# Projecting q, k and v in six chunks of 512 columns in place of eight of 384

## The chip, the core and the metric

The kernel runs on one core of a Trainium2 chip. The metric is the device time of one execution in microseconds; the times below are medians of several executions. The engines named are PE (TensorE, matmuls, with PEld for its weight loads), DVE (VectorE), ACT (ScalarE), POOL (GpSimd) and SP (SyncE), whose queue issues all the DMAs of this kernel.

## What is computed

Two mixers work on the same input x of 2048 rows by 1024 columns, in bf16, and a gate for each row mixes their results. Mixer A is a dilated local attention with 32 heads of 32 columns; each position looks at eight positions, itself and those 2, 4, ... 14 before it. Mixer B is a gated MLP with a spatial matmul.

```python
g = sigmoid((x * gate_w).sum(-1, keepdims=True))
qkv = (x @ wqkv)                       # 1024 x 3072: q, k, v of 32 heads
logits = einsum(q, k[s - 2*w]) * Dh ** -0.5,  w = 0..7, masked where s - 2*w < 0
a = (softmax(logits) applied to v[s - 2*w]) @ wo
z = gelu(x @ w_in);  z1, z2 = halves of z;  z2 = layernorm(z2)
b = (z1 * (w_sp @ z2 + b_sp)) @ w_out
out = g * a + (1 - g) * b
```

## The kernel before

**Stages on PE.** PE runs one matmul after another, in the order of the program. z2_quad and z2_tile (L223) make the first columns of z2 while x arrives. Then the projection (L431) makes q, k and v. Then the rest of z2 (L223), z1 (L473, 14 blocks f, each written out to z1_d), the spatial matmul in chunks (g_chunk, L487, 14 blocks f of 16 matmuls) and the output products (final_chunk, L509 with wo for a, L513 with w_out for b). The order of the chunks is g 0, g 1, final 0, g 2, final 1, g 3, final 2, final 3. All PE results go through one pool of eight PSUM tiles.

**The projection.** Heads are taken in eight groups of four, so a group has 128 columns each of q, k and v (C = 128). For each group g the loop at L423 goes over 16 row blocks j. A row block takes eight matmuls over kt, each 384 columns wide: q, k and v of the group next to each other in one PSUM tile. ACT casts the tile to bf16 into a stage slot (L434). After every four row blocks three DMAs (L440 to L442) store q, k and v to q_d, k_d and v_d in DRAM. The weights of a group lie in one of three slots wg_slots; a slot has four parts of 128 columns: q, k, v in the order the attention wants (columns by element, then head), and v as it was loaded. load_wg(g) loads the three blocks by three DMAs of 256 KB; v_order(g) reorders v on ACT (for the first group half on ACT, half on DVE). The weights of the next group but one are loaded when a group begins (L425), and the next group's v is reordered after row block 8.

**The attention.** It runs on DVE, group by group, while PE goes on with later stages. For a group, q, k and v are loaded back from DRAM (load_qk L309 and L310, load_v L313). Two halves jh of the rows are worked on one after the other: multiply (L266), four folds (L269) and a last add (L272) make the logits; then the soft_a part (L277 to L281), the exponential on ACT (L284), and soft_b (L287 to L291). The product with v of a group (L299, two folds L305 and L306, last add L302) runs one group later: after the logits of group g comes the product of group g-1. After the last group its own product follows. Outputs are stored to o_d in pairs of groups (store_o, L317). After the last store, wo is loaded (L357) and o_d is read back transposed, 128 rows at a time (load_oT, L360); the first such tile oT is read by the first matmul of final chunk 0.

**Other work on DVE.** Layer norm statistics (L365 to L369, with a power on POOL at L370), the normalization (L374), and in g_chunk for each f an add and a multiply on the evicted tile (L492 and L493, called a pair below; L491 is the cast on ACT before them, and three gsb slots lie between ACT and DVE). L493 reads z1c, which load_z1c (L391) loads from z1_d.

**What sets the order.** Each engine's queue and SP's queue run in the order in which the program emits instructions (`tc.manual_schedule`). A small planner, Beat, keeps a clock that each PE tile advances by its columns over 2360 a microsecond. Work for DVE is given with a start time and a length, DMAs and the exponential with a due time, and each is emitted when the clock reaches it (DVE work 3 us before, LEAD). The attention's first start is set from the length of one group's projection:

```python
QKV_US = NJ * KT * 3 * C * BEAT
beat.steps = attention_steps(beat.now + QKV_US + 10.0)
```

Loads of the attention are due at 1.0 us after the planned end of the last DVE work that reads what they overwrite, the store of o at 1.0 or 1.5 us, wo at 1.5 us and the first three oT at 8.0 us after the planned end. Other DMAs are emitted where they stand in the program: before g chunk 0, `load_z1c(0)`, the four transposing loads of w_sp for chunk 1 (load_wsp, L388), `load_z1c(1)` and w_out (L529); after g chunk 0 the four loads of w_sp for chunk 2; after g chunk 1 those for chunk 3, and then everything that is still due.

Of the kernel before, what the change touches and what calls it, by code (L numbers as in the profile page):

```python
# [13 lines left out]
P = 128  # L14
S = 2048
D = 1024
KT = D // P
NH = 32
DH = 32
HG = 4  # L20
NG = NH // HG
C = HG * DH
W = 8
NJ = 16
NJJ = NJ + 14
FH = 1792
# [4 lines left out]
EPS = 1e-5  # L31
SCALE = DH ** -0.5
WGS = 4 * KT * C
W2P = FH + 32
BEAT = 1.0 / 2360.0
LEAD = 3.0
# [4 lines left out]
CD_OFF = A_OFF + 22016  # L41
EF_OFF = CD_OFF + 19456
# [3 lines left out]
def _sub_ap(t, offset_elems, dims):  # L46
    return bass.AP(tensor=t.tensor, offset=t.offset + offset_elems, ap=[list(t.ap[0])] + [list(d) for d in dims])
# [3 lines left out]
def kernel(  # L51
# [13 lines left out]
    nc = tc.nc  # L65
# [10 lines left out]
    def reg(off, n):  # L76
        return arena[:, off:off + n]

    q_d = dpool.tile([NG, S, C], BF, name="q_d")
    k_d = dpool.tile([NG, S + 16, C], BF, name="k_d")  # L80
    v_d = dpool.tile([NG, S + 16, C], BF, name="v_d")
# [51 lines left out]
    ob_slots = [reg(A_OFF + 11264 + r * 1024, 1024) for r in range(3)]  # L133
    asb_slots = [reg(A_OFF + 14336 + r * 1024, 1024).bitcast(F32) for r in range(2)]
    w2 = reg(CD_OFF, KT * W2P).rearrange("p (k c) -> p k c", k=KT)
    stage_slots = [reg(CD_OFF + 14848 + r * 1536, 1536).rearrange("p (j c) -> p j c", j=4) for r in range(3)]
    wg_slots = [reg(EF_OFF + r * WGS, WGS).rearrange("p (t k c) -> p t k c", t=4, k=KT) for r in range(3)]
    junk = reg(EF_OFF + 3 * WGS, FH)
    w1_slots = [reg(EF_OFF + r * 4096, 4096).rearrange("p (k c) -> p k c", k=KT) for r in range(2)]
    z1s_slots = [reg(EF_OFF + 8192 + r * 2048, 2048).rearrange("p (c t) -> p c t", c=4) for r in range(2)]  # L140
    wsp_slots = [reg(CD_OFF, 8192).rearrange("p (i a t) -> p i a t", i=16, a=4),
# [7 lines left out]
    wq_v = A_wqkv.rearrange("(k p) c -> p k c", p=P)  # L149
# [5 lines left out]
    sync = nc.sync  # L155
# [37 lines left out]

    beat = Beat()

    def load_w(g, slot):
        part = 2 if slot == 3 else slot
        sync.dma_start(wg_slots[g % 3][:, slot, :, :], wq_v[:, :, part * D + g * C:part * D + (g + 1) * C])

    def load_wg(g):  # L200
        for slot in (3, 0, 1):
            load_w(g, slot)

    def v_order(g):
        wgt = wg_slots[g % 3]
        vdst = wgt[:, 2, :, :].rearrange("p k (d h) -> p k d h", d=DH, h=HG)
        vsrc = wgt[:, 3, :, :].rearrange("p k (h d) -> p k d h", h=HG, d=DH)
        if g == 0:
            nc.scalar.copy(vdst[:, 0:4], vsrc[:, 0:4])
            nc.vector.tensor_copy(vdst[:, 4:8], vsrc[:, 4:8])  # L210
        else:
            nc.scalar.copy(vdst, vsrc)

    def z2_tile(i, c):
        N = ZW[c] + 1 if c == 3 else ZW[c]
# [103 lines left out]
    def attention_steps(t):  # L319
        beat.at(t - 8.0, lambda: load_qk(0))  # L320
        beat.at(t - 7.9, lambda: load_v(0))
        for g in range(NG):
            for took, fn in qk_steps(0) + qk_steps(1):
                yield t, took, fn
            t = beat.vector
            if g + 1 < NG:
                beat.at(t + 1.0, lambda g=g: load_qk(g + 1))
            yield t, 2.4, soft_a
            t = beat.vector
            beat.at(t + (1.0 if g == 0 else 5.0), soft_exp)  # L330
            if g == 0:
                t += 5.0
            else:
                for took, fn in pv_steps(g - 1, 0) + pv_steps(g - 1, 1):
                    yield t, took, fn
                t = beat.vector
                if g + 1 < NG:
                    beat.at(t + 1.0, lambda g=g: load_v(g))
                else:
                    load_v(g)  # L340
                if g % 2 == 0:
                    beat.at(t + 1.5, lambda g=g: store_o(g - 1))
            yield t, 2.3, soft_b
            t = beat.vector
        for took, fn in pv_steps(NG - 1, 0) + pv_steps(NG - 1, 1):
            yield t + 5.0, took, fn
        t = beat.vector
        beat.at(t + 1.0, lambda: store_o(NG - 1))
        beat.at(t + 1.5, load_wo)
        for a in range(3):  # L350
            beat.at(t + 8.0, lambda a=a: load_oT(a))
# [46 lines left out]
        sync.dma_start(w2[:, kt, 0:2 * ZC], win_v[:, kt, FH:FH + 2 * ZC])  # L398
    for i in range(2, 16):
        if i == 14:  # L400
            load_w(0, 3)
            load_w(0, 0)
        sync.dma_start_transpose(xT[:, :, i * P:(i + 1) * P], x2[i * P:(i + 1) * P, :])
    load_w(0, 1)
    load_wg(1)
    for t_d in (k_d, v_d):
        sync.dma_start(bass.AP(tensor=t_d.tensor, offset=t_d.offset, ap=[[16, P], [(S + 16) * C, NG], [1, 16]]), zeros[:])
# [6 lines left out]
    for i in range(2, 16):  # L414
        if i == 14:
            v_order(0)
        z2_tile(i, 0)

    QKV_US = NJ * KT * 3 * C * BEAT
    beat.steps = attention_steps(beat.now + QKV_US + 10.0)  # L420

    stg = 0
    for g in range(NG):  # L423
        wgt = wg_slots[g % 3]
        if 0 < g and g + 1 < NG:  # L425
            load_wg(g + 1)
        for j in range(NJ):
            ps = psum.tile([P, 512], F32, name="ps", tag="ps")
            for kt in range(KT):
                lhsT = _sub_ap(xT_flat, kt * S + j, [[NJ, P]])  # L430
                nc.tensor.matmul(ps[:, 0:3 * C].rearrange("p (t c) -> p t c", t=3), lhsT, wgt[:, 0:3, kt, :],  # L431
                                 start=(kt == 0), stop=(kt == KT - 1))
            st = stage_slots[stg % 3]
            nc.scalar.copy(st[:, j % 4, :], ps[:, 0:3 * C])  # L434
            if j % 4 == 3:
                j0 = j - 3
                dq = bass.AP(tensor=q_d.tensor, offset=q_d.offset + (g * S + j0) * C, ap=[[NJ * C, P], [C, 4], [1, C]])
                dk = bass.AP(tensor=k_d.tensor, offset=k_d.offset + (g * (S + 16) + 16 + j0) * C, ap=[[NJ * C, P], [C, 4], [1, C]])
                dv = bass.AP(tensor=v_d.tensor, offset=v_d.offset + (g * (S + 16) + 16 + j0) * C, ap=[[NJ * C, P], [C, 4], [1, C]])
                sync.dma_start(dq, st[:, :, 0:C])  # L440
                sync.dma_start(dk, st[:, :, C:2 * C])
                sync.dma_start(dv, st[:, :, 2 * C:3 * C])  # L442
                stg += 1
            if j == 8 and g + 1 < NG:
                v_order(g + 1)
            beat.run(KT * 3 * C)

    load_w1(0)
    load_w1(1)
# [14 lines left out]
    for f in range(NF):  # L464
        ch = f // 4
# [4 lines left out]
        for c in range(4):  # L470
            ps = psum.tile([P, 512], F32, name="ps", tag="ps")
# [103 lines left out]
```

## Time and profile before

| | |
|---|---|
| Time, median of 3 runs | 716.57 us (716.35 to 716.60) |
| The profiled execution: time | 716.54 us |
| Its span | 714.7 us, granted clock 0.999 |
| PE busy | 706.6 us, 99% |
| DVE busy | 414.0 us, 58% |
| ACT busy | 251.3 us, 35% |
| L431, the projection on PE | 1024 matmuls of 128x384, 166.6 us busy |
| L487, the spatial matmul on PE | 128x512, 877 records, 192.9 us busy |
| L434, the casts of the projection on ACT | 128 of 128x384, mean 480 ns |
| L491, the casts of the spatial matmul on ACT | 56 of 128x512, mean 586 ns |
| ACT waiting for L431 | 87.2 us in 109 waits |
| Loads of wqkv | 24 of 256 KB, 4.6 us to landing |
| Stores of q, k, v | 32 each of 128 KB, 2.1, 2.2 and 2.5 us to landing |
| Loads of q, k, v for the attention | 512, 960 and 960 KB, 4.9, 6.8 and 5.4 us to landing |

The span is what the profiler saw between the first and the last instruction; the execution's time is 1.8 us longer. Times within a trace are counted from the span's start. A row of a group has the engine, the operation, what it writes and reads, the number of instructions, and then the busy time and the mean length of one. A matmul's mean length is its latency in the pipeline, so the distance between matmuls is read from busy time or from pieces of the chain. Some matmul records are missing (877 of 896 here). In the chain of work, a piece has its start, its length and the number of instructions in it. In a timeline the last bracket has the idle time before an instruction and what ended it. In rows on DMAs the last figure is the time from issue to landing.

### The profile page before, as it was taken

The page shows a single profiled execution, that of the slowest core. Times are in us where ns is not written, and L with a number is a line of the kernel's source. Part 1 is how long each engine was busy: PE and PEld are TensorE (multiplying, and loading weights), DVE is VectorE, ACT ScalarE, POOL GpSimd, SP SyncE. Part 2 cuts the span into 40 slices and gives each one's busy share as a digit, 9 for nine tenths or more (in the row PEclk, how much of TensorE's full clock was granted, in tenths as well). Part 3 has the DMA queues.
Part 4 walks back from the last instruction along what each step waited for, and adds up shares of the span by engine and source line. Part 5 has one row for each costly group of instructions (what it writes and reads, how often), then busy time and mean ns, then how long its engine had stood idle before and what let it go on. Part 6 is the DMA issues. An engine that isn't in the chain of part 4 may idle for free.

```text
span 714.7 us, 8897 instructions
## 1 busy us (share of the span) xinstructions
PE 706.6 (99%) x3577; PEld 402.0 (56%) x3628; DVE 414.0 (58%) x429; ACT 251.3 (35%) x483; POOL 11.0 (2%) x23
## 2 busy tenths in 40 slices
PE   8999999999999999999999999999999999999998
PEld 4488888888865554444444444444444444444444
DVE  0000989999999999999997999211222112221111
ACT  4444454445379894353521211111111111121111
POOL 1000000000000102000000000000000000000000
PEclk9999999999999999999999999999999999999999
DMA  9967776667781206954569580772400213002310
GB/s 238 191 149 220 165 200 170 167 133 193 202 237 66 85 1 181 253 184 137 173 196 293 213 174 2 220 146 59 133 1 0 55 49 119 1 1 59 60 45 29
DMA packets 176761, 92.93 MB, mean 130 GB/s; under 512 B 145104, under 2 KB 166992, under 8 KB 176208
## 3 DMA queue, kind: packets, MB, share of 16 engines
q1 hardware_dynamic: 176720, 92.36, 48.9%
q8 instruction: 28, 0.46, 0.3%
q14 instruction: 13, 0.11, 0.0%
HBM read 47.71 MB, written 28.38 MB: 106 GB/s over the span
## 4 chain that ended last, share of the span: by engine, by line
PE 98%; DMA 1%; issue 0%; SPq 0%; DVE 0%; DVEq 0%
PE ps L487 27%; PE ps L431 23%; PE ps L223 14%; PE ps L473 13%; PE psb L513 13%; PE psa L509 8%; DMA arena<-in_B_w_in_dram 1%; SPq L396 0%; DVE arena L517 0%; DVEq L517 0%
## 5 line engine op out<-in xcount | busy, mean ns | idle before, releaser
L487 PE MATMUL ps<-arena 128*128 128x512 bf16 x877 | 192.9, 379 | 1.0
L431 PE MATMUL ps<-arena 128*128 128x384 bf16 x1024 | 166.6, 326 | 0.0
L431 PEld LDWEIGHTS <-arena 128*128 128x128 bf16 x1024 | 147.6, 144 | 18.9
L487 PEld LDWEIGHTS <-arena 128*128 128x128 bf16 x896 | 87.7, 98 | 105.7
L513 PE MATMUL psb<-arena 128*128 128x512 bf16 (+1 forms) x455 | 101.3, 372 | 0.3
L223 PE MATMUL ps<-arena 128*128 128x512 bf16 (+1 forms) x501 | 96.7, 352 | 1.8 <-DMA arena<-in_B_w_in_dram 1.2
L517 DVE SCALAR_TENSOR_TENSOR arena<-psb,omg,arena 128x512 bf16<-128x512 f32 (+1 forms) x33 | 24.3, 735 | 125.4 <-PE psb L513 113.4
L473 PE MATMUL ps<-arena 128*128 128x512 bf16 x439 | 96.4, 379 | 0.5
L266 DVE TENSOR_TENSOR arena<-arena 128x8192 bf16<-128x8192 bf16 x16 | 70.8, 4423 | 43.1 <-DMA arena<-k_d 42.8
L434 ACT CAST arena<-ps 128x384 bf16<-128x384 f32 x128 | 60.5, 480 | 90.2 <-PE ps L431 87.2
L491 ACT CAST arena<-ps 128x512 bf16<-128x512 f32 x56 | 32.8, 586 | 163.4 <-PE ps L487 136.9
L269 DVE TENSOR_TENSOR arena<-arena 128x4096 bf16<-128x4096 bf16 (+1 forms) x64 | 77.7, 1214 | 1.9
L223 PEld LDWEIGHTS <-arena 128*128 128x128 bf16 x512 | 50.1, 98 | 48.0 <-issue 1.3
L513 PEld LDWEIGHTS <-arena 128*128 128x128 bf16 x462 | 45.2, 98 | 51.5
L473 PEld LDWEIGHTS <-arena 128*128 128x128 bf16 x448 | 43.9, 98 | 52.6
L299 DVE TENSOR_TENSOR arena<-arena,att_A 128x8192 bf16<-128x8192 bf16 x16 | 70.7, 4422 | 0.2
L492 DVE TENSOR_TENSOR arena<-arena 128x512 bf16<-128x512 bf16 x56 | 23.6, 422 | 77.9 <-ACT arena L491 77.9
L516 ACT ACTIVATE arena<-psa,g_s 128x512 f32<-128x512 f32 (+1 forms) x33 | 22.2, 674 | 122.3 <-PE psa L509 118.2
L509 PE MATMUL psa<-arena 128*128 128x512 bf16 (+1 forms) x259 | 60.2, 372 | 0.4
L475 ACT ACTIVATE arena<-ps 128x512 bf16<-128x512 f32 x56 | 33.1, 596 | 55.5 <-PE ps L473 49.3
L509 PEld LDWEIGHTS <-arena 128*128 128x128 bf16 x264 | 25.8, 98 | 29.7
L228 ACT ACTIVATE arena<-ps 128x512 bf16<-128x512 f32 (+1 forms) x64 | 34.2, 538 | 23.4 <-PE ps L223 22.1
(54 smaller groups left out, 254.0 us busy)
## 6 DMA issues: line engine op xcount, KB each, us to landing
arena<-k_d SPq DMA_DIRECT2D x8, 960.0 KB, 6.8
arena<-v_d SPq DMA_DIRECT2D x8, 960.0 KB, 5.4
z_d<-arena SPq DMA_DIRECT2D x14, 512.0 KB, 3.3
arena<-z_d SPq DMA_DIRECT2D x4, 1792.0 KB, 7.5
arena<-in_A_wqkv_dram SPq DMA_DIRECT2D x24, 256.0 KB, 4.6
arena<-in_B_w_in_dram SPq DMA_DIRECT2D x4, 1024.0 KB, 7.2
q_d<-arena SPq DMA_DIRECT2D x32, 128.0 KB, 2.1
k_d<-arena SPq DMA_DIRECT2D x32, 128.0 KB, 2.2
```

What stands on the lines that cost most here:

```text
L223: nc.tensor.matmul(ps[:, 0:N], xT[:, kt, i * P:(i + 1) * P], w2[:, kt, ZC * c:ZC * c + N], start=(kt == 0), stop=(kt == KT - 1))
L228: nc.scalar.activation(z2[:, i, ZC * c:ZC * c + n], ps[:, 0:n], ACT.Gelu_apprx_tanh, accum_out=s1[:, 4 * i + c:4 * i + c + 1])
L266: TT(prod.rearrange("p (w j c) -> p w j c", w=W, j=8, c=C), in0, in1, ALU.mult)
L269: return lambda: TT(pv[:, :, 0:half], pv[:, :, 0:half], pv[:, :, half:2 * half], ALU.add)
L299: TT(prod.rearrange("p (w j d h) -> p w j d h", w=W, j=8, d=DH, h=HG), in0, in1, ALU.mult)
L431: nc.tensor.matmul(ps[:, 0:3 * C].rearrange("p (t c) -> p t c", t=3), lhsT, wgt[:, 0:3, kt, :], start=(kt == 0), stop=(kt == KT - 1))
L434: nc.scalar.copy(st[:, j % 4, :], ps[:, 0:3 * C])
L473: nc.tensor.matmul(ps[:], w1[:, kt, (f % 4) * P:(f % 4 + 1) * P], xT[:, kt, 512 * c:512 * (c + 1)], start=(kt == 0), stop=(kt == KT - 1))
L475: nc.scalar.activation(z1s[:, c, :], ps[:], ACT.Gelu_apprx_tanh)
L487: nc.tensor.matmul(ps[:], z2[:, i, f * P:(f + 1) * P], wsp[:, i, :, :].rearrange("p a t -> p (a t)"), start=(i == 0), stop=(i == 15))
L509: nc.tensor.matmul(psa[:, 0:nw], oT[:, kt, :], wo_sb[:, kt, n0:n0 + nw], start=(kt == 0), stop=(kt == KT - 1))
L513: nc.tensor.matmul(psb[:, 0:nw], z1c[:, f, aa * P:(aa + 1) * P], w_out_sb[:, f, n0:n0 + nw], start=(f == 0), stop=(f == NF - 1))
```

## The change

The 24 blocks of 128 columns (q, k, v of group 0, then of group 1, and so on) are taken four at a time: six chunks ch of 512 columns. Chunk 0 has q, k, v of group 0 and q of group 1; chunk 1 has k, v of group 1 and q, k of group 2; chunk 2 has v of group 2 and q, k, v of group 3; chunks 3 to 5 go on in the same way with groups 4 to 7. So chunks 2 and 5 have two v blocks, the others one.

A row block now takes eight matmuls of 512 columns, one cast of 512 columns and, after every four row blocks, four stores in the order of the blocks. There are two weight slots of four blocks in place of three, and three separate slots for v as loaded. The stage slots are larger, and one of them is placed in another region. A chunk's loads take its v blocks first. The planner's length of a chunk is that of 512 columns. Attention, z2, z1, g_chunk and final_chunk are not edited.

```diff
+NCH = 3 * NG // 4
...
-    stage_slots = [reg(CD_OFF + 14848 + r * 1536, 1536).rearrange("p (j c) -> p j c", j=4) for r in range(3)]
-    wg_slots = [reg(EF_OFF + r * WGS, WGS).rearrange("p (t k c) -> p t k c", t=4, k=KT) for r in range(3)]
-    junk = reg(EF_OFF + 3 * WGS, FH)
+    stage_slots = [reg(off, 2048).rearrange("p (j c) -> p j c", j=4)
+                   for off in (CD_OFF + 14592, CD_OFF + 16640, EF_OFF + 13056)]
+    wg_slots = [reg(EF_OFF + r * WGS, WGS).rearrange("p (t k c) -> p t k c", t=4, k=KT) for r in range(2)]
+    vraw_slots = [reg(EF_OFF + 2 * WGS + r * KT * C, KT * C).rearrange("p (k c) -> p k c", k=KT) for r in range(3)]
+    junk = reg(EF_OFF + 2 * WGS + 3 * KT * C, FH)
...
+    def blocks(ch):
+        return [divmod(b, 3) for b in range(4 * ch, 4 * ch + 4)]
+
+    def load_w(ch, pos):
+        g, part = blocks(ch)[pos]
+        dst = vraw_slots[g % 3] if part == 2 else wg_slots[ch % 2][:, pos, :, :]
+        sync.dma_start(dst, wq_v[:, :, part * D + g * C:part * D + (g + 1) * C])
+
+    def load_wg(ch):
+        for pos in sorted(range(4), key=lambda p: blocks(ch)[p][1] != 2):
+            load_w(ch, pos)
+
+    def v_order(ch):
+        for pos, (g, part) in enumerate(blocks(ch)):
+            if part != 2:
+                continue
+            vdst = wg_slots[ch % 2][:, pos, :, :].rearrange("p k (d h) -> p k d h", d=DH, h=HG)
+            vsrc = vraw_slots[g % 3].rearrange("p k (h d) -> p k d h", h=HG, d=DH)
...
         if i == 14:
-            load_w(0, 3)
+            load_w(0, 2)
             load_w(0, 0)
...
     load_w(0, 1)
+    load_w(0, 3)
     load_wg(1)
...
-    QKV_US = NJ * KT * 3 * C * BEAT
+    QKV_US = NJ * KT * 4 * C * BEAT
...
+    def store_rows(st, ch, j0):
+        for pos, (g, part) in enumerate(blocks(ch)):
+            t_d, rows, first = ((q_d, S, 0), (k_d, S + 16, 16), (v_d, S + 16, 16))[part]
+            dst = bass.AP(tensor=t_d.tensor, offset=t_d.offset + (g * rows + first + j0) * C, ap=[[NJ * C, P], [C, 4], [1, C]])
+            sync.dma_start(dst, st[:, :, pos * C:(pos + 1) * C])
...
+    for ch in range(NCH):
+        wgt = wg_slots[ch % 2]
+        if 0 < ch and ch + 1 < NCH:
+            load_wg(ch + 1)
         for j in range(NJ):
...
-                nc.tensor.matmul(ps[:, 0:3 * C].rearrange("p (t c) -> p t c", t=3), lhsT, wgt[:, 0:3, kt, :],
+                nc.tensor.matmul(ps[:].rearrange("p (t c) -> p t c", t=4), lhsT, wgt[:, :, kt, :],
...
-            nc.scalar.copy(st[:, j % 4, :], ps[:, 0:3 * C])
+            nc.scalar.copy(st[:, j % 4, :], ps[:])
             if j % 4 == 3:
...
+                store_rows(st, ch, j - 3)
                 stg += 1
-            if j == 8 and g + 1 < NG:
-                v_order(g + 1)
-            beat.run(KT * 3 * C)
+            if j == 8 and ch + 1 < NCH:
+                v_order(ch + 1)
+            beat.run(KT * 4 * C)
```

More of the change, by code (lines that the diff above doesn't have):

```diff
@@ L194 @@
     beat = Beat()
[L196 to L212, printed above, removed]
+    def blocks(ch):
[13 more added lines that the diff above has]
+            vsrc = vraw_slots[g % 3].rearrange("p k (h d) -> p k d h", h=HG, d=DH)
+            if ch == 0:
+                nc.scalar.copy(vdst[:, 0:4], vsrc[:, 0:4])
+                nc.vector.tensor_copy(vdst[:, 4:8], vsrc[:, 4:8])
+            else:
+                nc.scalar.copy(vdst, vsrc)
     def z2_tile(i, c):
@@ L417 @@
         z2_tile(i, 0)
-    QKV_US = NJ * KT * 3 * C * BEAT
+    QKV_US = NJ * KT * 4 * C * BEAT
     beat.steps = attention_steps(beat.now + QKV_US + 10.0)
     stg = 0
[L423 to L426, printed above, removed]
+    def store_rows(st, ch, j0):
[7 more added lines that the diff above has]
+            load_wg(ch + 1)
         for j in range(NJ):
@@ L430 @@
                 lhsT = _sub_ap(xT_flat, kt * S + j, [[NJ, P]])
-                nc.tensor.matmul(ps[:, 0:3 * C].rearrange("p (t c) -> p t c", t=3), lhsT, wgt[:, 0:3, kt, :],
+                nc.tensor.matmul(ps[:].rearrange("p (t c) -> p t c", t=4), lhsT, wgt[:, :, kt, :],
                                  start=(kt == 0), stop=(kt == KT - 1))
             st = stage_slots[stg % 3]
-            nc.scalar.copy(st[:, j % 4, :], ps[:, 0:3 * C])
+            nc.scalar.copy(st[:, j % 4, :], ps[:])
             if j % 4 == 3:
[L436 to L442, printed above, removed]
+                store_rows(st, ch, j - 3)
                 stg += 1
-            if j == 8 and g + 1 < NG:
-                v_order(g + 1)
-            beat.run(KT * 3 * C)
+            if j == 8 and ch + 1 < NCH:
+                v_order(ch + 1)
+            beat.run(KT * 4 * C)
     load_w1(0)
```

## The prediction

> **What bounds the kernel now.** I read the chain that ended last first, then its pieces in order of time, then the timelines of DVE and of the SP queue.
>
> ```profile
> PE 98%; DMA 1%; issue 0%; SPq 0%; DVE 0%; DVEq 0%
> ...
> 37.29 166.40 PE ps L431 x1024
> ...
> 375.16 10.74 PE ps L487 x49
> 385.95 10.74 PE ps L487 x49
> ```
>
> PE is the chain. The whole projection is one piece of 166.40 us without a hole, 162.5 ns for each of 1024 matmuls. So a gain can only come from fewer PE nanoseconds, and a loss from anything that makes PE wait. The attention on DVE runs beside PE, and its end is the place to look at:
>
> ```profile
> 71.89 4.43 DVE L266 TENSOR_TENSOR arena<-arena 128x8192 bf16<-128x8192 bf16 x1 [42.25 <-DMA arena<-k_d]
> ...
> 379.60 0.43 DVE L493 TENSOR_TENSOR arena<-arena 128x512 bf16<-128x512 bf16 x1 [4.28 <-DMA arena<-z_d]
> ...
> 397.47 4.42 DVE L299 TENSOR_TENSOR arena<-arena,att_A 128x8192 bf16<-128x8192 bf16 x1
> ...
> 423.01 4.42 DVE L299 TENSOR_TENSOR arena<-arena,att_A 128x8192 bf16<-128x8192 bf16 x1
> ...
> 444.65 0.69 DVE L302 TENSOR_TENSOR arena<-arena 128x1024 bf16<-128x1024 bf16 x1
> ```
>
> DVE starts when the first k lands, has almost no idle time from 71.9 to 445.3 but the 4.28 us for the first z1c, and ends the attention at 445.3. What hangs on that end is on SP:
>
> ```profile
> 387.52 0.43 SPq L529 DMA_DIRECT2D arena<-in_B_w_out_dram  x1
> 412.77 0.32 SPq L313 DMA_DIRECT2D arena<-v_d  x1
> 414.64 11.64 SPq L388 DMA_TRANSPOSE arena<-in_B_w_sp_dram  x4
> 445.36 0.57 SPq L317 DMA_DIRECT2D o_d<-arena  x1
> 446.03 5.04 SPq L357 DMA_DIRECT2D arena<-in_A_wo_dram  x4
> 451.17 7.24 SPq L360 DMA_TRANSPOSE arena<-o_d  x3
> ```
>
> ```profile
> arena<-o_d SPq DMA_TRANSPOSE x1, 7.0
> ```
>
> ```profile
> 462.79 1.89 PE L509 MATMUL psa<-arena 128*128 128x512 bf16 x8
> ```
>
> The second fence is the DMA view at 451.1: the first oT is 7.0 us from issue to landing, so it is there at 458.2, 12.9 us after DVE's last attention instruction. PE wants it at 462.79. The margin is 4.6 us, and everything below is held against it.
>
> **The matmuls: -0.67 us on the path.** Columns are the same (1024 x 384 = 768 x 512). L487's two pieces start 10.79 us apart; taken as 50 matmuls with one record missing that is 215.8 ns. A check: 2 x 14 x 16 = 448 of them lie between 366.26 and 462.95, 96.7 us, again 215.8. So 768 x 215.8 = 165.73 against 166.40. The strided weight loads (142 to 151 ns in L431's row) fitted under 162.5 ns and fit under 215.8.
>
> **ACT, weights, stores: 0, with the cover named.** Casts are 128 x 480 = 61.4 us before and 96 x 586 (L491's row, same shape) = 56.3 after, on an engine that waited 87.2 us for PE here. The v copies (2.0 us each) stay eight on ACT and DVE together; two now stand in a row in chunks 1 and 4, 4 us against eight PSUM tiles of 8 x 215.8 ns = 13.8 us. Weight loads stay 24 and stores 96. With two slots, the load for chunk c+1 overwrites chunk c-1, but on SP it stands behind c-1's last stores, which wait for its last cast, so the new PE wait is met when SP comes to it. Behind it stand q/k/v loads and stores, for which three stage slots last two times 6.9 us. The cover is a chunk of 27.6 us against four issues (0.82 each at 60.22) and 4.6 to landing, 7.9; if the cover went, that much per chunk. At the start the fourth block takes the place of the next group's first load, issued about 31.0, 4.7 to landing: 35.7 against PE's 37.1. I take 0, bounds 0 and 1 (one more issue ahead of it).
>
> **The attention starts later.** Chunk 0 has 128 x 215.8 = 27.6 us, not 20.8: +6.8. One store more and one load more lie on SP ahead of the first q/k (0.5 + 0.8), and 256 KB + 128 KB more ahead of them in the DMA queue. That order holds there:
>
> ```profile
> q_d<-arena SPq DMA_DIRECT2D x1, 128.0 KB, 10.1
> ```
>
> This store, issued at 64.55 behind k and v, took 10.1 us where its median is 2.1. First k: about 80.4 instead of 71.7, and group 1's k now also comes behind four weight loads. Delay 8.9; bounds 6.8 (only the chunk) and 9.8.
>
> DVE then comes to group 7's first mul at 366.25 + 8.9 - 0.4 = 374.8 (half of the 0.9 us wait for rstd goes). By the order of instructions in the changed kernel the first two L492/L493 pairs follow this mul directly; before, three folds (4.2 us) stood ahead of the first pair. So the z1c wait of 4.28 us, over at about 379 in both, swallows half of the delay, and from there DVE has 4.2 us more attention and, by the same order, 23 instead of 21 pairs (0.8 each) before its end: 65.7 + 4.2 + 1.6 = 71.5, from 379.9 to 451.4. If nothing else comes, the attention ends 6.1 late.
>
> **Two v loads move past slow transfers on SP.** The planner's times move by 27.76 - 20.82 = 6.94 us, and the order of SP shows what that does. (1) v of group 6 stood at 360.5, before the first z1c load; now it stands after L388's four transposes, the second z1c and the 3.58 MB of w_out, which took 17.2 us to land (issued 387.52). SP also comes there some 2.8 us sooner, as the last z1 store no longer queues behind an o store. So w_out is in at 402 to 404, and v, 960 KB at the 3 us or so that it takes beyond an empty queue's latency, at 405 to 407. DVE wants it at 403.5 (walk: 379.9, pairs 0 to 7, two muls and folds, soft_a). Bounds 0 and 4 us. (2) v of group 7 stood at 412.77, ahead of the four transposes; now behind them: 414.64 - 0.67 + 11.64 = 425.6. Alone it took 5.0 (its own row); the last transpose, landing 4.9 after its issue, is still ahead. It is in at 430.6 to 432. DVE wants it at 429.7, or up to 433.7 if it has lost 4 us at (1): the two waits don't add up. I take 432 for the first mul of group 7's pv. From there to the end are two muls, their folds and six pairs, 21.7 us: **453.7**, 8.4 late; bounds 451.2 and 455.5.
>
> **The sum.** 453.7 + 12.9 = 466.6 for oT. PE wants it at 462.79 - 0.67 = 462.1. Stall 4.5 us, bounds 2.0 and 6.3. Nothing gives it back: PE's later chunks run without holes, and of what follows on SP (next transposes of w_sp, needed a chunk later) nothing is near. The profiled execution was 716.54 (span 714.7), 0.03 under the median of 716.57: 716.54 - 0.67 + 4.5 = **720.4**, bounds 717.9 and 722.2.
>
> A PE hole of this length has no row here. The rows nearest to it are the beginning of the span:
>
> ```profile
> 2.02 0.15 PEld L91 LDWEIGHTS <-warm 128*128 128x128 bf16 x1 [0.28 <-issue]
> 2.44 0.15 PEld L91 LDWEIGHTS <-warm 128*128 128x128 bf16 x1 [0.28 <-issue]
> ```
>
> The same 512-column matmul is spaced 0.42 us there and 0.216 later; the slow stretch is over by 4.8 us at the latest, so 3.6 us of it at half speed lost at most 1.8. A hole of 1.20 us at 4.85 brought no slow stretch back. So after my hole: 0 to 1.8 us more; I take 0, as nothing shows a fall back, and 1.8 on the upper bound: 724.0.
> [...]
>
> **Rivals.**
> R1, the margin holds: the attention ends by 449.2 (4.6 - 0.67 after 445.3), PE never waits, and only the matmuls count: 716.54 - 0.67 = 715.9. Up to 451.3 it stays within 0.2%. For it: DVE's own work alone would end at 451.4, and at 449.3 with the delay at its lower bound. Against it: v of group 7 cannot be issued before PE leaves the first g chunk. It decides only if that load lands by 429.6, in 4 us, where the fastest v load took 4.5.
> R2, hole plus clock: the stall is at its upper half (5.5) and the slow stretch comes back (1.8): 723.2. For it: the start of the span. Against it: no slow PE slice anywhere later, but also no hole.
> R3, the changed weight loading stalls PE too: two slots and four loads in a row. Price one late block a chunk boundary, about 1 us x 6: with the stall 726. Against it: 20 us of cover.
> R4, faster by over 0.2% (below 715.1): needs 0.8 us beyond the matmul gain in a chain with 1% of non-PE time, and no stall. Nothing shows it.
>
> **Numbers.** Forecast 0.60, R1 0.17 (715 to 718), R2 0.16, R3 0.04, R4 0.03. A measurement of this kernel can tell about 0.2% (1.4 us) from no change, so the bounds are 715.1 and 718.0. Faster 0.04, same 0.18, slower 0.78. The range 717.2 to 724 leaves out most of R1, R3 and R4; the forecast's own is 717.9 to 722.2.
>
> **What would show it.** L431's successor as one piece of 165.7 us; the first attention mul at about 80.5; v of group 7 issued after the four transposes near 425.6 and waited for; the last attention instruction at 453 to 454; and the first psa matmul with a wait of some 4.5 us for oT's DMA. I am wrong if that group has no wait, if PE waits in the projection, or if the matmuls there are not spaced 215.8 ns.

## The result and the profile after

| | before | after |
|---|---|---|
| Time, median | 716.60 us (716.35 to 718.78, 6 runs) | 721.01 us (719.48 to 722.55, 6 runs) |
| Ratio, 95% interval | | 1.0063 (1.0050 to 1.0075) |
| The profiled execution | 716.54 us, span 714.7, granted clock 0.999 | 722.27 us, span 720.5, granted clock 0.995 |

The changed kernel is slower by 4.4 us. Its profiled execution is one of its two longest. Of the six, the two at a granted clock of 0.995 took 722.3 and 722.6 us, the three at 0.997 and 0.998 took 720.6 to 721.2, and the one at 1.000 took 719.5. This spread of 3 us is explained below.

The page of the kernel after, with the shares of the chain that ended last and three groups of instructions (line, engine, operation, operands, count, then busy time and mean ns of one, then idle time before and its releaser):

```profile
PE 35%; DVE 10%; DMA 2%; issue 0%; DVEq 0%
...
L447 PE MATMUL ps<-arena 128*128 128x512 bf16 x768 | 165.9, 379 | 0.0
...
L447 PEld LDWEIGHTS <-arena 128*128 128x128 bf16 x768 | 110.7, 144 | 55.1
...
L450 ACT CAST arena<-ps 128x512 bf16<-128x512 f32 x96 | 55.9, 589 | 92.7 <-PE ps L447 87.1
```

The projection does what the change says: 768 matmuls, no idle time before them, and weight loads and casts that fit beside them. But PE, which made up 98% of the span in the chain before, makes up 35% now. (The shares add to 47%, as the chain can be followed back only to 381 us.) Read backwards, the chain leaves PE at one place and goes on through DVE, so something held PE up. Its pieces in order of time (start, length, what) show where, in the kernel after:

```profile
452.38 0.69 DVE arena L311
...
453.10 6.13 DMA o_d<-arena
...
459.24 6.28 DMA arena<-o_d
...
465.62 3.57 PE psa L519 x8
469.19 4.28 PE psb L523 x14
473.47 1.73 PE psa L519 x8
475.20 3.02 PE psb L523 x14
```

The attention's last instruction ends at 453.07, then its output is stored and read back transposed, and final chunk 0 starts at 465.62, 12.55 us later. PE's previous work ended at 462.29: a hole of 3.33 us. After it come two slow pieces. Eight psa matmuls take 3.57 us where the same first piece took 1.89 before, and fourteen psb matmuls take 4.28 where the next fourteen take 3.02. These are 1.68 + 1.26 = 2.94 us more. The account for this execution is then -0.67 + 3.33 + 2.94 = 5.60 us of the 5.73 between the two profiled executions.

Why the pieces are slow is read from the windows of the kernel after. The columns are the stretch, its length, PE's busy time and number of instructions, the granted clock, the DMA share and GB/s:

```profile
462.00:465.60 3.60, 0.29 (x2) 0.89 1.15 331
465.60:469.20 3.60, 3.58 (x9) 0.50 1.05 165
469.20:473.50 4.30, 4.30 (x15) 0.72 1.17 247
473.50:478.20 4.70, 4.70 (x23) 1.00 0.78 168
```

After the hole the granted clock is 0.50, then 0.72 on the mean of the next stretch, then full again.

On DVE's timeline of the kernel after (start, length, instruction, idle time before and its releaser) the attention's lateness can be followed:

```profile
80.14 4.43 DVE L275 TENSOR_TENSOR arena<-arena 128x8192 bf16<-128x8192 bf16 x1 [49.88 <-DMA arena<-k_d]
...
107.67 4.43 DVE L275 TENSOR_TENSOR arena<-arena 128x8192 bf16<-128x8192 bf16 x1 [1.74 <-DMA arena<-k_d]
...
376.75 4.42 DVE L275 TENSOR_TENSOR arena<-arena 128x8192 bf16<-128x8192 bf16 x1
...
405.10 4.42 DVE L308 TENSOR_TENSOR arena<-arena,att_A 128x8192 bf16<-128x8192 bf16 x1
...
431.30 4.42 DVE L308 TENSOR_TENSOR arena<-arena,att_A 128x8192 bf16<-128x8192 bf16 x1
```

The second and third of these, group 1's first multiply and group 7's, in the kernel before:

```profile
98.32 4.42 DVE L266 TENSOR_TENSOR arena<-arena 128x8192 bf16<-128x8192 bf16 x1 [0.56 <-DMA arena<-k_d]
...
366.25 4.42 DVE L266 TENSOR_TENSOR arena<-arena 128x8192 bf16<-128x8192 bf16 x1
```

Against the kernel before (71.89, 98.32, 366.25, 397.47, 423.01) the five are late by 8.25, 9.35, 10.5, 7.6 and 8.3 us. The step from 8.25 to 9.35 is group 1's k, waited for 1.74 us in place of 0.56. Of the step to 10.5, 0.9 is a second wait for the layer norm's power on POOL (one wait of 0.9 us before, two now). The drop from 10.5 to 7.6 is the wait for the first z1c, 4.28 us before, which is gone, less two more L502 and L503 pairs that fall into this stretch (eight for six, 0.8 us each). Neither product of the last two groups (405.10, 431.30) waits for its v. What SP did in that time, in the kernel after:

```profile
369.71 13.46 SPq L397 DMA_TRANSPOSE arena<-in_B_w_sp_dram  x4
383.21 0.58 SPq L400 DMA_DIRECT2D arena<-z_d  x1
383.84 0.43 SPq L539 DMA_DIRECT2D arena<-in_B_w_out_dram  x1
384.32 7.41 SPq L322 DMA_DIRECT2D arena<-v_d  x1
...
413.97 10.24 SPq L397 DMA_TRANSPOSE arena<-in_B_w_sp_dram  x4
424.32 0.52 SPq L322 DMA_DIRECT2D arena<-v_d  x1
```

and in the DMA view of the kernel after at 384.3 the load of v for group 6 (last figure, us to landing):

```profile
arena<-v_d SPq DMA_DIRECT2D x1, 960.0 KB, 19.8
```

Behind w_out this load lands at 404.1, one microsecond before DVE is free for it. The one of group 7, issued at 424.32 and 5.0 us to landing, is in at 429.3, two before DVE comes. So in this kernel DVE's own lateness and the two loads end within 2 us of each other, and which of them counts can't be read from it. That is what most of the experiments are for.

### The profile page after: what moved, and what is told of

Read it like the earlier page. It is cut to its first block, busy times and chain, and to the rows that moved or that the text cites. A ratio compares the mean times of both kernels' runs of the same rounds, so it can differ in the third digit from the quotient of the medians.

```text
span 720.5 us, 8378 instructions
## 1 busy us (share of the span) xinstructions
PE 711.8 (99%) x3372; PEld 365.8 (51%) x3372; DVE 413.7 (57%) x429; ACT 246.3 (34%) x451; POOL 14.0 (2%) x23
## 5 line engine op out<-in xcount | busy, mean ns | idle before, releaser
L497 PE MATMUL ps<-arena 128*128 128x512 bf16 x896 | 193.9, 379 | 0.0
L447 PE MATMUL ps<-arena 128*128 128x512 bf16 x768 | 165.9, 379 | 0.0
L497 PEld LDWEIGHTS <-arena 128*128 128x128 bf16 x896 | 87.7, 98 | 105.7
L447 PEld LDWEIGHTS <-arena 128*128 128x128 bf16 x768 | 110.7, 144 | 55.1
L523 PE MATMUL psb<-arena 128*128 128x512 bf16 (+1 forms) x462 | 103.4, 376 | 0.0
L483 PE MATMUL ps<-arena 128*128 128x512 bf16 x448 | 96.9, 379 | 0.0
L501 ACT CAST arena<-ps 128x512 bf16<-128x512 f32 x56 | 32.9, 587 | 162.0 <-PE ps L497 129.4
L450 ACT CAST arena<-ps 128x512 bf16<-128x512 f32 x96 | 55.9, 589 | 92.7 <-PE ps L447 87.1
L232 PEld LDWEIGHTS <-arena 128*128 128x128 bf16 x512 | 50.1, 98 | 48.0 <-issue 1.2
L523 PEld LDWEIGHTS <-arena 128*128 128x128 bf16 x462 | 45.6, 99 | 52.8 <-issue 2.2
L483 PEld LDWEIGHTS <-arena 128*128 128x128 bf16 x448 | 43.8, 98 | 52.7
L519 PE MATMUL psa<-arena 128*128 128x512 bf16 (+1 forms) x264 | 62.3, 380 | 3.3 <-DMA arena<-o_d 3.3
L502 DVE TENSOR_TENSOR arena<-arena 128x512 bf16<-128x512 bf16 x56 | 23.6, 422 | 72.1 <-ACT arena L501 72.1
L519 PEld LDWEIGHTS <-arena 128*128 128x128 bf16 x264 | 26.1, 99 | 34.1 <-issue 5.4
```

Source lines behind the costliest of these rows:

```text
L232: nc.tensor.matmul(ps[:, 0:N], xT[:, kt, i * P:(i + 1) * P], w2[:, kt, ZC * c:ZC * c + N], start=(kt == 0), stop=(kt == KT - 1))
L447: nc.tensor.matmul(ps[:].rearrange("p (t c) -> p t c", t=4), lhsT, wgt[:, :, kt, :], start=(kt == 0), stop=(kt == KT - 1))
L450: nc.scalar.copy(st[:, j % 4, :], ps[:])
L483: nc.tensor.matmul(ps[:], w1[:, kt, (f % 4) * P:(f % 4 + 1) * P], xT[:, kt, 512 * c:512 * (c + 1)], start=(kt == 0), stop=(kt == KT - 1))
L497: nc.tensor.matmul(ps[:], z2[:, i, f * P:(f + 1) * P], wsp[:, i, :, :].rearrange("p a t -> p (a t)"), start=(i == 0), stop=(i == 15))
L501: nc.scalar.copy(gsb, ps[:])
```

## The experiments

**Theory.** The wide matmul gives 0.67 us. The loss comes from the attention's later end, by two causes of about equal size: the first k comes later, and the planner's later times put two v loads behind slow DMAs. PE's hole then costs its length, and some executions pay a slow clock on top. **Rivals:** the width itself costs something; only DVE's lateness counts; only the loads count.

**1. The planner's number alone, in the kernel before.** Matmuls stay 384 wide.

```diff
-    QKV_US = NJ * KT * 3 * C * BEAT
+    QKV_US = NJ * KT * 4 * C * BEAT
```

> The kernel before with one number changed: the planner is told that the first group takes 512 columns' time, so the attention is planned 6.94 us later; matmuls, casts, stores and weight slots are those of before. Theory (the loss of the change is the later attention, which makes PE wait for the first oT): the first k is in some 4 us later (no weight loads ahead of it), v of group 7 goes behind the four transposes of w_sp as in the changed kernel, is in at about 430 and is waited for; the attention ends near 452, and the first psa matmul waits 1 to 3 us: 717.6 to 720. Rival (the loss comes with the wide matmuls, the four loads and stores or the two weight slots): no change, 716.4 to 716.8.

Measured: 721.29 us (719.49 to 721.40, 5 runs), ratio 1.0061 (1.0048 to 1.0073). The direction was the theory's, the size was larger than expected. DVE's timeline and PE's in this kernel:

```profile
100.96 0.43 DVE L287 TENSOR_TENSOR att_m<-att_L 128x256 f32<-128x256 f32 x1 [4.59 <-ACT att_L L284]
...
405.26 4.42 DVE L299 TENSOR_TENSOR arena<-arena,att_A 128x8192 bf16<-128x8192 bf16 x1 [3.74 <-DMA arena<-v_d]
```

```profile
465.85 2.36 PE L509 MATMUL psa<-arena 128*128 128x512 bf16 x8 [2.88 <-DMA arena<-o_d]
468.00 4.44 PE L513 MATMUL psb<-arena 128*128 128x512 bf16 x14
```

k comes only 1.7 us later here (73.56). But ACT's exponential is emitted by the planned time, so DVE loses 4.59 us to it, and v of group 6, behind w_out, makes DVE wait 3.74. The attention ends at 453.2, the hole is 2.88 us, and the slow matmuls follow. A loss as large as the whole change's comes without one wide matmul: the width is not needed for it. The way to it is not quite the same, as DVE loses its time here to the exponential more than to k.

**2. The hole given other work.** The kernel after; in the first row block of final chunk 0 both psb products are put ahead of the psa products, which need oT.

```diff
...
+                if a > 0:
+                    psa = mm_a(oT, n0, nw)
+                    psb = mm_b(z1c, aa, n0, nw)
+                elif n0 == 0:
+                    early = [mm_b(z1c, aa, m0, 512) for m0 in (0, 512)]
+                    psa, psb = mm_a(oT, n0, nw), early[0]
+                else:
+                    psa, psb = mm_a(oT, n0, nw), early[1]
...
```

mm_a and mm_b hold the two loops of matmuls as they were.

> The changed kernel, but in final chunk 0 the two psb products of the first row block are put ahead of its psa products. Theory: PE has 28 matmuls of 215.8 ns = 6.0 us of work before it needs the first oT, the hole of 3.3 us is covered and no slow matmuls follow: 716.6 - 0.7 = 715.9, from 715.6 to 716.2, all executions within 0.5. Rival (the loss is somewhere else, for instance in the projection or in DMA contention): 720 to 722 as before this edit.

Measured: 716.00 us (715.32 to 718.13, 11 runs) against 716.53 (21 runs), ratio 0.9995 (0.9986 to 1.0004). PE's timeline of this kernel:

```profile
462.50 6.21 PE L517 MATMUL psb<-arena 128*128 128x512 bf16 x28
468.54 5.34 PE L510 MATMUL psa<-arena 128*128 128x512 bf16 x23
```

The attention still ends at 453.7, and nothing waits for it. So all of the loss passes through this one hole. What is left of the change lies between -1.0 and +0.3 us, and the 0.67 of the matmuls are within that.

**3. The hole filled with useless matmuls.** The kernel after; 14 matmuls on a zero tile (warm_up, the function that starts the kernel) between g chunk 1 and final chunk 0. They write a PSUM tile that nothing reads. They leave the wait for oT as it is.

```diff
+    warm_up(14)
```

> The changed kernel with 14 more matmuls on the zeroed warm tile (3.0 us, nothing reads them) between g chunk 1 and final chunk 0, where PE otherwise waits. Theory of two parts (the wait itself, 3.3 us, and then matmuls at half speed because PE had been idle): the wait for oT stays where it was, the slow matmuls go: 719.2 to 719.8, executions within 0.5 of each other, clock 0.999 or more. Rival (the long psa and psb matmuls after the wait come from their data, wo or the next oT landing late): 721 with the same spread of 3 us, the first psa group still twice as long.

Measured: 719.37 us (718.65 to 719.86, 5 runs), clock 1.000 in all five, ratio 1.0041 (1.0027 to 1.0054). PE's timeline of this kernel:

```profile
461.93 3.19 PE L92 MATMUL pw<-warm 128*128 128x512 bf16 x14
465.85 1.89 PE L519 MATMUL psa<-arena 128*128 128x512 bf16 x8 [0.73 <-DMA arena<-o_d]
```

psa starts no earlier than in the kernel after, yet takes 1.89 us again. This takes the two costs apart: 719.37 - 716.53 + 0.67 = 3.5 us is the wait itself, and the 1.6 us to the median of the kernel after is the slow clock, 0 to 3 us by execution.

**4. Wide matmuls without the later start.** The kernel after with chunks of 3, 4, 4, 4, 3, 3 and 3 blocks. The first chunk and the planner's length are those of the kernel before.

```diff
-NCH = 3 * NG // 4
+WIDTHS = (3, 4, 4, 4, 3, 3, 3)
+NCH = len(WIDTHS)
...
-    QKV_US = NJ * KT * 4 * C * BEAT
+    QKV_US = NJ * KT * WIDTHS[0] * C * BEAT
...
```

> The changed kernel with seven chunks of 3, 4, 4, 4, 3, 3 and 3 blocks in place of six of 4: two weight slots, four loads and four stores at a time as in the change, but the first chunk, and with it the planner's number, is again 384 columns. Theory: the first k is in at about 73 (one load more ahead of it), the attention ends within 2 us of 445.3, no wait for oT, and the matmuls are 512 x 162.5 + 384 x 215.8 = 166.07 us, 0.33 less than before: 716.0 to 716.5. Rival (slots, loads or stores of the change cost the time): 718 to 721.

Measured: 716.20 us (715.61 to 718.57, 11 runs), ratio 0.9999 (0.9990 to 1.0007). DVE's first multiply and its last add in this kernel:

```profile
72.30 4.42 DVE L277 TENSOR_TENSOR arena<-arena 128x8192 bf16<-128x8192 bf16 x1 [42.63 <-DMA arena<-k_d]
...
446.50 0.68 DVE L313 TENSOR_TENSOR arena<-arena 128x1024 bf16<-128x1024 bf16 x1
```

With the first k back at 72.3 the attention ends at 447.2 and there is no hole. Three wide chunks, two weight slots and blocks of two groups in one chunk cost nothing that shows: the interval is -0.7 to +0.5 us.

**5 to 7. Which of the two ties.** Theory A says that DVE's lateness and v of group 6 behind w_out are a tie, so that taking away one alone brings nothing. B says that the lateness alone counts, C that the load alone does. Three versions of the kernel after. In the first, the weights of the next chunk are loaded after row block 4 and not at the chunk's start, so that group 1's q and k don't queue behind them:

```diff
-        if 0 < ch and ch + 1 < NCH:
-            load_wg(ch + 1)
...
+            if j == 4 and 0 < ch and ch + 1 < NCH:
+                load_wg(ch + 1)
```

> The changed kernel with the weight loads of each following chunk issued at row block 4 of a chunk in place of its beginning, so the first loads of q, k and v go ahead of them; the order on DVE, ACT and of all later loads is unchanged. Theory A (what the attention's end hangs on after 380 us is two things that tie: DVE's own lateness, and v of group 6 behind w_out, in at 404.1 in the changed kernel against DVE at 405.1): the first k is in some 5 us earlier, at about 75, the exponential planned on ACT gives part of that back, and the attention ends only about 1 us earlier, 452, with DVE now waiting for v of group 6: hole 2.3 us, 718.5 to 721.5. Theory B (the late first k alone sets the end): the end comes forward by the whole 3 to 5 us, no hole, 716.

In the second, w_out is loaded after block 8 of g chunk 0, behind v:

```diff
+            if c == 0 and f == 8:
+                sync.dma_start(w_out_sb, B_w_out.rearrange("(f p) n -> p f n", p=P))
...
-    sync.dma_start(w_out_sb, B_w_out.rearrange("(f p) n -> p f n", p=P))
```

> The changed kernel with the load of w_out issued after block 8 of g chunk 0 in place of ahead of that chunk. Theory A: v of group 6 is in 10 us earlier, but DVE comes to it at 405 by its own work, so nothing moves: attention end 453, 719.5 to 722.5. Theory C (v of group 6 behind w_out alone sets the end): the end comes forward by several us, 716 to 718.

The third has both edits.

> The changed kernel with both edits, weights later and w_out later. Theory A: with both out of the way the next limit is v of group 7 behind the four transposes, in at 429.3; its product starts near 429.5 in place of 431.3, the attention ends near 451.2, a hole of about 1.5 us and no slow matmuls: 717.0 to 718.3. If the transposes don't matter either: end below 449.5, 715.9.

| | median (lowest to highest, runs) | ratio (interval) | product of group 6 starts | hole |
|---|---|---|---|---|
| after | 721.01 (719.48 to 722.55, 6) | 1.0063 (1.0050 to 1.0075) | 405.10 | 3.33 us |
| weights later | 719.38 (719.17 to 720.46, 4) | 1.0047 (1.0032 to 1.0062) | 405.22 | 3.19 us |
| w_out later | 721.00 (719.45 to 725.40, 5) | 1.0083 (1.0056 to 1.0109) | 405.19 | 3.29 us |
| both | 717.50 (716.99 to 718.66, 10) | 1.0018 (1.0009 to 1.0028) | 401.32 | 1.72 us |

The kernel before took 716.25 us (14 runs) beside these three. The last two columns are read from the profiled executions. The timelines of DVE and PE of the first, weights later:

```profile
405.22 4.43 DVE L308 TENSOR_TENSOR arena<-arena,att_A 128x8192 bf16<-128x8192 bf16 x1 [3.09 <-DMA arena<-v_d]
...
465.75 1.89 PE L519 MATMUL psa<-arena 128*128 128x512 bf16 x8 [3.19 <-DMA arena<-o_d]
```

Of the second, w_out later, and then its DMA view at 384.6:

```profile
405.19 4.42 DVE L308 TENSOR_TENSOR arena<-arena,att_A 128x8192 bf16<-128x8192 bf16 x1
...
465.74 1.89 PE L521 MATMUL psa<-arena 128*128 128x512 bf16 x8 [3.29 <-DMA arena<-o_d]
```

```profile
arena<-v_d SPq DMA_DIRECT2D x1, 960.0 KB, 10.5
```

And DVE's of the third, both:

```profile
401.32 4.42 DVE L308 TENSOR_TENSOR arena<-arena,att_A 128x8192 bf16<-128x8192 bf16 x1
...
429.15 4.43 DVE L308 TENSOR_TENSOR arena<-arena,att_A 128x8192 bf16<-128x8192 bf16 x1 [1.54 <-DMA arena<-v_d]
```

With the weights later, the first k comes at 77.38 in place of 80.14, DVE is there three microseconds earlier, and waits them out for v. With w_out later, v takes 10.5 us to landing in place of 19.8 and DVE comes no earlier. Either alone leaves the product at 405.2 and the hole as it was; B and C fall. Only both together move it, by 3.8 us, and then the next tie shows: v of group 7, behind the transposes, takes 1.54 back.

The medians of the first two differ by 1.6 us, though the holes of their profiled executions are equal. Their clocks account for most of it: three of the four executions of the first ran at 0.999 or 1.000, four of the five of the second at 0.998 or less. One of these, 725.40 us at 0.995, is some 3 us longer than the two executions of the kernel after at that clock; why is not known.

**8. The plan moved back, a miss.** The kernel after, planned 2.5 us earlier, so that both v loads stand on SP where they stood before the change.

```diff
-    beat.steps = attention_steps(beat.now + QKV_US + 10.0)
+    beat.steps = attention_steps(beat.now + QKV_US + 7.5)
```

> The changed kernel with one number changed: the attention is planned 7.5 us after the end of chunk 0 in place of 10. By its order of instructions this puts the first q, k and v ahead of the weight loads, v of group 6 back ahead of the first z1c load, v of group 7 back ahead of the four transposes, and 22 pairs in place of 23 ahead of the attention's end. Theory: the attention ends near 448, the first oT is in before PE wants it (462.1), no hole, no slow matmuls: 715.7 to 716.3. Rival (a chunk of 27.6 us makes the attention too late whatever the plan): end at 451 or later, 717.5 or more.

Measured: 727.80 us (727.05 to 728.22, 4 runs), ratio 1.0160 (1.0145 to 1.0175), clock 0.993 in all four. The forecast was wrong by some 12 us. SP's timeline of this kernel, then DVE's:

```profile
370.05 0.33 SPq L322 DMA_DIRECT2D arena<-v_d  x1
374.36 0.57 SPq L326 DMA_DIRECT2D o_d<-arena  x1
375.03 1.61 SPq L487 DMA_DIRECT2D z_d<-arena  x1
381.38 0.33 SPq L400 DMA_DIRECT2D arena<-z_d  x1
```

```profile
388.57 0.43 DVE L503 TENSOR_TENSOR arena<-arena 128x512 bf16<-128x512 bf16 x1 [7.33 <-DMA arena<-z_d]
```

The order did come back, but the engine did not: the first k was there at 75.70, and group 1's k, behind four weight loads, made DVE wait 6.32 us. v and the store of o wait for DVE on SP's queue, DVE is late against this plan, and behind them stand the last store of z1 and the load of z1c. That load is issued at 381.38 in place of 369.33, DVE stands 7.33 us for it, the attention ends at 459.2, and the hole is 9.5 us. PE's wait (total, times, longest), and then the first piece behind it in the chain:

```profile
PE psa L519 <- DMA arena<-o_d: 9.5, 1, 9.5
```

```profile
471.79 3.41 PE psa L519 x8
```

In the kernel after, the later plan is what keeps SP from standing behind a late DVE; the fault is in what stands ahead of the two loads.

**9. All three causes out.** The version with both edits, and the four transposes of w_sp issued after block 4 of g chunk 1, behind v of group 7.

```diff
+            if c == 1 and f == 4:
+                for aa in range(4):
+                    load_wsp(2, aa)
...
-    for aa in range(4):
-        load_wsp(2, aa)
...
```

> The changed kernel with three edits: weights later and w_out later as in the run with both, and the four transposes of w_sp for chunk 2 issued after block 4 of g chunk 1, so v of group 7 goes ahead of them. Theory: each of the three was the next limit; the wait of 1.54 us for v of group 7 goes too, the attention ends near 449.4, the first oT is in at about 462, a hole of at most 0.5 us: 715.7 to 716.5. Rival (something else holds the attention's end at 451): 717.5 again.

Measured: 715.93 us (715.39 to 718.06, 11 runs) against 716.44 (21 runs), ratio 0.9995 (0.9986 to 1.0004). The timelines of SP, DVE and PE of this kernel:

```profile
417.35 0.32 SPq L322 DMA_DIRECT2D arena<-v_d  x1
...
427.38 4.42 DVE L308 TENSOR_TENSOR arena<-arena,att_A 128x8192 bf16<-128x8192 bf16 x1
...
458.77 2.97 PE L497 MATMUL ps<-arena 128*128 128x512 bf16 x13
461.68 1.89 PE L524 MATMUL psa<-arena 128*128 128x512 bf16 x8
```

v of group 7 goes out at 417.35, its product starts at 427.38 without a wait, the attention ends at 449.1, and final chunk 0 follows g chunk 1 without a hole. With these three queueings gone the loss is gone, to within the interval (-1.0 to +0.3 us).

**10. The same, with psb first as in experiment 2.**

> The three edits and the psb products of the first row block ahead of its psa products. Theory: no hole and 4 to 6 us of cover for oT, only the gain of the matmuls is left: 715.6 to 716.1, 0.1% under before.

Measured: 715.71 us (715.15 to 716.21, 11 runs), ratio 0.9987 (0.9978 to 0.9996) to the kernel before on the same chip. It is the only version here whose interval lies below 1, and PE is 99% of its chain. The gain, 0.73 us by the medians (0.3 to 1.6 by the interval), is the size of the matmuls' 0.67.

## Why the prediction was right, and where not

**The matmuls: right.** In the chain of experiment 9's kernel, which runs through PE again, the projection is one piece of 165.76 us against 166.40 before: -0.64 for the -0.67 worked out.

**ACT, weights, stores at nothing: right.** No PE wait in the projection, casts 55.9 us for the 56.3 expected; R3 did not come. Experiment 4 shows the same of the slots and blocks.

**The attention's start: right.** 80.14 for 80.5. The delay in the sum, 8.9 us, was a little long: it was 8.25. Of the 8.9 (8.7 by the prediction's own 80.4 against 71.7), 6.8 + 0.5 + 0.8 = 8.1 were worked out; no row gives the rest.

**DVE's lateness at group 7: mis-sized.** It was taken as 8.5 us (a start at 374.8) and was 10.5 (376.75). The step that failed let half of a rstd wait disappear, where a second one came (0.9 us), and put no price on group 1's k, though it named it: that k makes DVE later by another 1.1 us. The walk that came after was right: from the first L503 (381.60) to the attention's end DVE took 71.5 us, as worked out without the two v waits.

**The two v loads: issued as forecast, and costing nothing here.** Group 6's landed at 404.1, 2.3 us behind w_out (issued at 383.84, 18.0 us to landing) and a little ahead of the forecast 405 to 407, group 7's at 429.3 for 430.6 to 432. I had DVE wait 2.3 us for them together; a DVE later by 2 us did not wait. The end, 453.07 for 453.7, came out right by two errors of about equal size and opposite sign, which is luck. The statement that the two waits don't add up could not show in this kernel, where neither came. Experiment 5 bears it out: there DVE loses 3.09 us to group 6's v and then begins group 7's product, at 431.43, without a wait. It holds for DVE's lateness too: experiments 5 to 7 show a tie that a single edit doesn't open.

**The stall: 3.33 for 4.5 us.** 0.6 of the difference is the attention's end, 0.4 the way from there to oT (12.55 for 12.9; the transposed load landed in 6.3 us, not 7.0), 0.2 PE coming later (462.29 for 462.1).

**The clock: the wrong end of the bounds.** I took 0 from 0 to 1.8. The runs gave 0 to 3, and 2.9 in the profiled one. The row that I judged by, a hole of 1.20 us without a slow stretch, was too short to tell; the hole of 1.72 us in experiment 7 brought none either. R2's mechanism came, in five of six executions at least in part (clocks of 0.995 to 0.998), though its other half, a stall of 5.5, did not. In the profiled execution the granted clock was 1.00 before the hole of 3.33 us, 0.50 for 6.8 us from a point within it on, and 1.00 again later (see the last section). A hole of 2.88 us in experiment 1 was followed by slow matmuls as well: in its chain eight psa took 2.36 us and fourteen psb 4.24, for 1.89 and 3.02 at 1.00. So holes shorter than the 4.5 us that I forecast were followed by a slow stretch.

**The sum.** 716.57 - 0.67 + 3.33 = 719.2, and the rest to 721.0, 1.8 us, is the clock. The forecast of 720.4 was near since a stall 1.2 us too long stood for a clock at 0. The mechanism, the place and the sign were right. That the number was within 0.6 us is luck in part, as two mis-sized terms cancelled.

**R1** fell with the margin of 4.6 us less 0.67, against an end 7.7 us later. Experiments 4 and 9, which keep the end at 447.2 and 449.1, show that its bound, 449.2, was drawn in the right place, and experiment 7, with its end at 450.9 and a hole of 1.72, gives 449.2 again. **R4** did not come.

## What to carry to other kernels

A gain on the engine that is the bound can be lost through the size of the first piece, as everything that waits for that piece starts later, and through a planner that moves all due times with it: after such a change, look on each queue for loads that now stand behind large or slow ones. When two latenesses end within a microsecond or two, taking away one shows nothing, so test both together before calling either harmless. And look for DMAs that wait for an engine: in experiment 8 the load of z1c stood on SP's queue behind such waits and went out at 381.38 in place of 369.33. Planning them earlier than the engine comes can cost more than planning them late, there 727.80 us against 721.01. Where the order of a product is free, put what depends on late data last; here it made the kernel indifferent to the whole question.

## What the runs showed of the hardware

After a PE hole of 2.9 to 3.3 us the granted clock fell in some executions and not in others of the same kernel: in experiment 1 the clock was 0.998 in three executions and 1.000 in two, in experiment 5 0.997 in one and 0.999 or 1.000 in three. The profiled executions of the kernel after (3.33 us) and of experiment 1 (2.88) have slow matmuls behind the hole, at a cost of 2.9 and 1.7 us; those of experiments 5 and 6 (3.19 and 3.29) have none. After 9.5 us (experiment 8) all four executions had a clock of 0.993; after 1.72 us (experiment 7) and 0.73 us (experiment 3) the clock of every execution was 0.999 or 1.000.

In the kernel after, the windows above (a mean of 0.89 between 1.00 and 0.50 is 0.50 for 2 x 0.11 of the time) give 2 x 0.11 x 3.60 + 3.60 + 2 x 0.28 x 4.30 = 6.8 us at 0.50. Windows of 0.25 us put its ends at 464.8 and 471.6. That is twice as long as in experiment 1, where the clock was 0.69 on the mean from 465.80 to 469.20 and 0.80 from 469.20 to 472.50: 2 x 0.31 x 3.40 + 2 x 0.20 x 3.30 = 3.4 us at 0.50, from about 467.1 to 470.5. For experiment 8 the mean clock of the execution gives an estimate of 2 x 0.007 x 725.2, some 10 us at 0.50. In the kernel after PE has matmuls in 6.0 us of its low stretch, and about half of that, 2.9 us, was lost. The hole of 9.5 us cost only 1.5 us of slow matmuls (3.41 us for the first eight psa in place of 1.89), less than the hole of 3.33; by the same estimate most of its low stretch lay in the hole itself. The mean clocks of the three profiled executions, 0.998, 0.995 and 0.993 for 3.4, 6.8 and some 10 us, count the hole too (0.5 x 6.8 of 720.5 is 0.0047). The six executions of the kernel after: one at 1.000 took 719.5 us, three at 0.997 and 0.998 were 1.1 to 1.7 us longer, and two at 0.995 were 2.8 to 3.1 longer.

In the kernel after, the clock fell 2.5 us after PE had stopped, within the hole; in experiment 1 it fell some 1.2 us after PE had resumed. How much idle time is enough, and what decides between the executions at 3 us, is not settled by these runs.

The same 960 KB landed at different times by what stood ahead of them on the queue: 19.8 us behind the 3.58 MB of w_out, 10.5 us ahead of it but behind the load of z1c (experiment 6), and 5.0 us behind four transposes of w_sp alone.
